# One decode step, forward and backward: attention output and query gradient in one pass over the cache slots

## The chip, the core and the metric

The kernel runs on one core of a Trainium2 chip. The metric is the time of one execution on the device in microseconds (us). The kernel before takes 334.01 us in the median of three runs (333.45 to 334.48). The execution that the profiler recorded spans 335.7 us; all stage times below are from it.

## The reference

A decode step with one new token for each of B = 4 sequences: attention over a cache and a gated feed-forward layer, added to the input, and then all gradients. Cut to what matters:

```python
xn = layernorm(x)                                   # x: [4, 1, 512]
# A: attention over the last W = 1024 of 4096 cache slots, 32 query heads on 8 key/value heads
q = (xn @ wq).reshape(B, 1, 32, 128).transpose(0, 2, 1, 3)
k = repeat(k_cache[:, :, Sk - W:, :], 4, axis=1)    # caches: [4, 8, 4096, 128]
v = repeat(v_cache[:, :, Sk - W:, :], 4, axis=1)
p = softmax(einsum("bhqd,bhkd->bhqk", q, k) * 128 ** -0.5)
o = einsum("bhqk,bhkd->bhqd", p, v)                 # contraction over the slots
a = o.transpose(0, 2, 1, 3).reshape(B, 1, 4096) @ wo
# B: feed-forward, F = 1792
f = (gelu(xn @ w_gate) * (xn @ w_up)) @ w_down
out = x + a + f
# outputs: out and the gradients of x, k_cache, v_cache, wq, wo, w_gate, w_up, w_down for grad_out
```

All arrays are bf16. The gradients of the two caches are zero outside the last 1024 slots, and those zeros have to be written too. In the backward pass `dq` is a contraction over the slots, as `o` is: `dq = dS @ k`, with `dS` the gradient of the scores. The weight gradients are outer products with a contraction over the four sequences only: `dwo` from `o` and `grad_out`, `dwq` from `xn` and `dq`, and those of the feed-forward layer from its rows and `grad_out` or `xn`.

## The kernel before

The kernel first does the feed-forward layer, and then four steps t = 0 to 3 of GP = 2 key/value heads each (HG = 8 query heads). A scheduler of the framework orders each engine's instructions; the program below gives the priorities. Weight gradients and cache gradients are cut into pieces that wait in a list `bg`; `tick(n)` takes the next n of them at fixed places between other work.

```python
J, JQ, rep = 32, 8, 4          # 1024 slots of 4 sequences: 32 blocks of 128 rows per key/value head

od_ps = ps_a.tile([P, 2, GP, Dh], FP32, name="od_ps")     # kept for the whole kernel
# copies of grad_out and of xn, row p kept only where its head of four is i
for src, dst in ((dy_b, dym), (xn_b, xnm)):
    for i in range(rep):
        nc.vector.tensor_scalar(out=dst[:, i, :], in0=src[:], scalar1=msk_i[:, i:i + 1], ...)
...
def scores(t, k):                      # k = 0: S = q k^T;  k = 1: dP = do v^T
    for g in range(GP):
        for q in range(NQ):
            # 8 transposes of 128x128 into T_ps, one copy T_sb, and then
            for b in range(B):         # four PE column groups
                nc.tensor.matmul(ps[b * RG:(b + 1) * RG, :], lhsT=lf[:, b, s * RG:(s + 1) * RG],
                                 rhs=T_sb[:, :, b], ..., tile_position=(0, b * RG))
            tick(2)
...
def by_batch(src, nm):                 # spreads 256 columns over 4 sequences: 1024 columns, on GpSimd
    dst = attw.tile([P, JQ, P], BF16, name=nm, ...)
    nc.gpsimd.tensor_tensor(out=..., in0=src[:].unsqueeze(2).broadcast_to([P, WQ, B]),
                            in1=bmsk[:].unsqueeze(1).broadcast_to([P, WQ, B]), op=ALU.mult)
# softmax:   P_b -> P_x = by_batch(P_b)  -> eight transposes pT_ps -> copy PT
# softmax_d: dS_b -> dS_x = by_batch(dS_b) -> eight transposes pT_ps -> copy dST
...
def odq(t, k):                         # k = 0: o = P v;  k = 1: dq = dS k
    pT, blks = st[t][("PT", "dST")[k]], (v_t, k_t)[k]
    for g in range(GP):
        for j in range(J):
            nc.tensor.matmul(od_ps[0:rep * B, k, g, :], lhsT=pT[:, j % JQ, j // JQ, g], rhs=blks[(t, g)][:, j, :],
                             start=(j == 0), stop=(j == J - 1))
    rows = attw.tile([P, GP, Dh], BF16, name="od_r", ...)
    # k = 0: vector copy of od_ps; k = 1: ScalarE copy with the scale
    # two transposes odT_ps, copy od_T
...
def dw(t):
    # piece_o: dwo of one head: o_r[:, g, :] against dym[:, i, :], 512 columns, 8 pieces
    # piece_q: dwq: two matmuls of 256 columns, xnm against dq_r, 8 pieces
...
def f_rows(srcT, nm):                  # rows of the feed-forward layer, four blocks of 128 per matmul
    ps = od_ps[:].rearrange("p k g d -> p (k g) d")
    for f4 in range(NF4):              # NF4 = 4
        nc.tensor.matmul(ps[0:4 * B, f4, :], lhsT=srcT[:, 4 * f4:4 * f4 + 4, :]..., rhs=ident[:], ...)
    evac(rows[:], ps, 512)
...
for t in range(NT):                    # NT = 4
    if t == 0:
        pre(t)                         # q and do of the step, from transposed wo and from wq
    masks(t)                           # domr, qmr on GpSimd: the right sides of dv and dk
    scores(t, 0)
    softmax(t)
    dvdk(t, 0)                         # puts 16 pieces into the list
    scores(t, 1)
    softmax_d(t)
    dvdk(t, 1)                         # 16 pieces
    odq(t, 0)
    if t + 1 < NT:
        pre(t + 1)
    odq(t, 1)
    fin(t)                             # o @ wo, and dq against transposed wq
    load_next(t)                       # loads of step t + 2
    dw(t)                              # 16 pieces
```

The zeros of the cache gradients (50 MB) are written by large transfers that are issued at fixed places of the program, each behind a ScalarE copy.

Of the kernel before, what the change touches and what calls it, by code (L numbers as in the profile page):

```python
# [14 lines left out]
P = 128  # L15
# [3 lines left out]
def kernel(  # L19
# [113 lines left out]
    msk_i = const.tile([P, rep], FP32, name="msk_i")  # L133
    nc.vector.reduce_sum(out=msk_i[:], in_=ident_f[:].rearrange("p (r b) -> p r b", b=B)[:, 0:rep, :], axis=AX.X)
# [34 lines left out]

    acc = const.tile([P, 2, ND, B], FP32, name="acc")  # L170
# [14 lines left out]
    od_ps = ps_a.tile([P, 2, GP, Dh], FP32, name="od_ps")  # L185
# [27 lines left out]
    xnm = const.tile([P, rep, D], BF16, name="xnm")  # L213
    dym = const.tile([P, rep, D], BF16, name="dym")
    for src, dst in ((dy_b, dym), (xn_b, xnm)):
        for i in range(rep):
            nc.vector.tensor_scalar(out=dst[:, i, :], in0=src[:], scalar1=msk_i[:, i:i + 1], scalar2=None,
                                    op0=ALU.mult)
# [99 lines left out]
    def masks(t):  # L318
        for k, nm in enumerate(("do", "q")):
            mr = attw.tile([P, GP, NQ, Dh], BF16, name=nm + "mr", tag=nm + "mr")  # L320
            nc.gpsimd.tensor_tensor(out=mr[:].rearrange("p g q d -> p (g q) d"),
                                    in0=st[t]["r4"][:, k, :].unsqueeze(1).broadcast_to([P, NS, Dh]),
                                    in1=msk[:].rearrange("p g q -> p (g q)").unsqueeze(2).broadcast_to([P, NS, Dh]),
                                    op=ALU.mult)
            st[t][nm] = mr
# [23 lines left out]
    def by_batch(src, nm):  # L349

        dst = attw.tile([P, JQ, P], BF16, name=nm, tag=nm, bufs=1)
        nc.gpsimd.tensor_tensor(out=dst[:].rearrange("p j (m b) -> p (j m) b", b=B),  # L352
                                in0=src[:].unsqueeze(2).broadcast_to([P, WQ, B]),
                                in1=bmsk[:].unsqueeze(1).broadcast_to([P, WQ, B]), op=ALU.mult)
        return dst
# [12 lines left out]
    def softmax(t):  # L368
# [24 lines left out]
        P_x = by_batch(P_b, "P_x")  # L393
        st[t].update(E=E_f, rr=rr, PT=transposed(P_x, "PT"), P=P_x)

    def softmax_d(t):
        E_f, rr, dP = st[t]["E"], st[t]["rr"], st[t]["dP"]
        Gt = attw.tile([P, WQ], FP32, name="Gt", tag="Gt", bufs=1)
        gs = attw.tile([P, 1], FP32, name="gs", tag="gs")
        nc.vector.tensor_tensor_reduce(out=Gt[:], in0=E_f[:], in1=dP, scale=1.0, scalar=0.0,  # L400
                                       op0=ALU.mult, op1=ALU.add, accum_out=gs[:])
        gs_ps = ps_x.tile([P, 1], FP32, name="gs_ps", tag="x")
        nc.tensor.matmul(gs_ps[:], lhsT=rsum_f, rhs=gs[:], start=True, stop=True)
        cc = attw.tile([P, 1], FP32, name="cc", tag="cc")
        nc.vector.tensor_tensor(out=cc[:], in0=gs_ps[:], in1=rr[:], op=ALU.mult)
        nc.vector.scalar_tensor_tensor(out=Gt[:], in0=dP, scalar=cc[:, 0:1], in1=E_f[:],
                                       op0=ALU.subtract, op1=ALU.mult)
        dS_b = attw.tile([P, WQ], BF16, name="dS_b", tag="dS_b", bufs=1)
        nc.vector.tensor_scalar(out=dS_b[:], in0=Gt[:], scalar1=rr[:, 0:1], scalar2=None, op0=ALU.mult)  # L409
        dS_x = by_batch(dS_b, "dS_x")  # L410
        st[t].update(dST=transposed(dS_x, "dST"), dS=dS_x)

    def odq(t, k):

        pT, blks = st[t][("PT", "dST")[k]], (v_t, k_t)[k]
        for g in range(GP):
            for j in range(J):
                nc.tensor.matmul(od_ps[0:rep * B, k, g, :], lhsT=pT[:, j % JQ, j // JQ, g], rhs=blks[(t, g)][:, j, :],  # L418
                                 start=(j == 0), stop=(j == J - 1))
        rows = attw.tile([P, GP, Dh], BF16, name="od_r", tag=f"od_r{k}")  # L420
        if k == 0:
            nc.vector.tensor_copy(out=rows[:], in_=od_ps[:, k])
        else:
            nc.scalar.activation(out=rows[:], in_=od_ps[:, k], func=ACT.Copy, scale=scale)
        T_ps = ps_w.tile([P, GP, P], BF16, name="odT_ps", tag="w")
        for g in range(GP):
            nc.tensor.transpose(T_ps[:, g, :], rows[:, g, :], ident[:])
        rT = attw.tile([P, GP, rep, B], BF16, name="od_T", tag=f"od_T{k}")
        nc.vector.tensor_copy(out=rT[:],  # L429
                              in_=T_ps[:].rearrange("p g (r b) -> p g r b", b=B)[:, :, 0:rep, :])  # L430
        st[t][("o", "dq")[k]] = rows, rT
# [23 lines left out]
    def dw(t):  # L455

        o_r, dq_r = st[t]["o"][0], st[t]["dq"][0]

        def piece_o(g, i, held):
# [3 lines left out]
            nc.tensor.matmul(mps[:], lhsT=o_r[:, g, :], rhs=dym[:, i, :], start=True, stop=True)  # L463
            evac(held["osb"][:, i, :], mps[:], 512)
            if i == rep - 1:
                r0 = (t * HG + g * rep) * Dh
                store(nc.gpsimd, out=out_5[r0:r0 + rep * Dh, :].rearrange("(h p) n -> p h n", p=P),
                                    in_=held["osb"][:], kind="rest",
                          apart=["zeros", "rest"])

        def piece_q(c2, k, held):
            if k == 0:
                held["osb"] = outp.tile([P, 2, GP, rep, Dh], BF16, name="osb_q", tag="o")
            ci, i2 = k // 2, k % 2
            c = c2 * 2 + ci
            mps = ps_w.tile([P, 2, GP, Dh], FP32, name="dwq_ps", tag="w")
            for i in range(2):
                nc.tensor.matmul(mps[:, i].rearrange("p g d -> p (g d)"),  # L478
                                 lhsT=xnm[:, i2 * 2 + i, c * P:(c + 1) * P],
                                 rhs=dq_r[:].rearrange("p g d -> p (g d)"), start=True, stop=True)  # L480
            evac(held["osb"][:, ci, :, i2 * 2:(i2 + 1) * 2, :], mps[:].rearrange("p i g d -> p g i d"), 512)
            if k == 3:
                store(nc.gpsimd, out=out_4[c2 * 2 * P:(c2 + 1) * 2 * P, t * CW:(t + 1) * CW].rearrange("(c p) j -> p c j", p=P),
                    in_=held["osb"][:].rearrange("p c g i d -> p c (g i d)"), kind="rest",
                          apart=["zeros", "rest"])

        assert rep == 4
# [4 lines left out]
        for c2 in range(ND // 2):  # L492
            held = {}
            for k in range(4):
                bg.append(lambda c2=c2, k=k, held=held: piece_q(c2, k, held))

    def fin(t):

        oT, dqT = st[t]["o"][1], st[t]["dq"][1]
# [16 lines left out]
    NF4 = (NF + 3) // 4  # L516
# [9 lines left out]
    def ftb(name):  # L526
        t_ = ffn.tile([P, 4 * NF4, B], BF16, name=name)
        nc.vector.memset(t_[:], 0.0)
        return t_
# [53 lines left out]
    nc.vector.tensor_tensor(out=aT_b[:, 0:NF, :], in0=gl[:], in1=hu, op=ALU.mult)  # L583
    dhuT_b = ftb("dhuT_b")
    nc.vector.tensor_tensor(out=dhuT_b[:, 0:NF, :], in0=da[:], in1=gl[:], op=ALU.mult)
# [3 lines left out]
    nc.vector.tensor_tensor(out=dhgT_b[:, 0:NF, :], in0=dhg_f[:], in1=gp[:], op=ALU.mult)  # L589
# [3 lines left out]
    def f_rows(srcT, nm):  # L593

        ps = od_ps[:].rearrange("p k g d -> p (k g) d")
        for f4 in range(NF4):
            nc.tensor.matmul(ps[0:4 * B, f4, :], lhsT=srcT[:, 4 * f4:4 * f4 + 4, :].rearrange("p f b -> p (f b)"),
                             rhs=ident[:], start=True, stop=True)
        rows = const.tile([P, NF4, P], BF16, name=nm)
        evac(rows[:], ps, 512)  # L600
# [3 lines left out]
    def piece_d(f4, i, n, held):  # L604
# [3 lines left out]
        nc.tensor.matmul(mps[:], lhsT=a_r[:, f4, :], rhs=dym[:, i, :], start=True, stop=True)  # L608
        evac(held["osb"][:, i, :], mps[:], 512)
        if i == n - 1:  # L610
            store(nc.gpsimd, out=out_8[4 * f4 * P:(4 * f4 + n) * P, :].rearrange("(h p) n -> p h n", p=P),
                                in_=held["osb"][:, 0:n, :], kind="rest",
                      apart=["zeros", "rest"])

    def piece_g(s_r, og, c, i, held):
        if i == 0:
            held["osb"] = outp.tile([P, NF4, 4, P], BF16, name="osb_g", tag="o")
        n = (NF - i + 3) // 4
        mps = ps_w.tile([P, NF4, P], FP32, name="dwg_ps", tag="w")
        nc.tensor.matmul(mps[:, 0:n, :].rearrange("p f d -> p (f d)"), lhsT=xnm[:, i, c * P:(c + 1) * P],  # L620
                         rhs=s_r[:, 0:n, :].rearrange("p f d -> p (f d)"), start=True, stop=True)
        evac(held["osb"][:, 0:n, i, :], mps[:, 0:n, :], n * P)
        if i == 3:
            store(nc.gpsimd, out=og[c * P:(c + 1) * P, :],
                                in_=held["osb"][:].rearrange("p f i d -> p (f i d)")[:, 0:F], kind="rest",
                      apart=["zeros", "rest"])

    for f4 in range(NF4):
        held = {}
        n = min(4, NF - 4 * f4)  # L630
        for i in range(n):
            bg.append(lambda f4=f4, i=i, n=n, held=held: piece_d(f4, i, n, held))
# [3 lines left out]
    for srcT, wsb, og, nm in ((dhgT_b, wg_sb, out_6, "dhg_r"), (dhuT_b, wu_sb, out_7, "dhu_r")):  # L636
        s_r = f_rows(srcT, nm)
        for c in range(ND):
            held = {}
            for i in range(4):  # L640
# [20 lines left out]
    with tc.tile_pool(name="stage", bufs=3, reuse_waits="tile") as stage, \  # L661
# [6 lines left out]
        for t in range(NT):  # L668
# [10 lines left out]
            odq(t, 0)  # L679
# [3 lines left out]
            odq(t, 1)  # L683
# [67 lines left out]
```

## Time and profile before

| | us or share |
|---|---|
| time, median of 3 | 334.01 (333.45 to 334.48) |
| recorded span | 335.7 |
| TensorE (PE) busy | 241.3, 72% |
| VectorE (DVE) busy | 160.8, 48% |
| ScalarE (ACT) busy | 115.6, 34% |
| GpSimd (POOL) busy | 62.8, 19% |
| bytes moved by DMA | 112.38 MB, mean 335 GB/s |
| P_x of the four steps begins at | 73.8, 136.5, 201.2, 266.6 |
| dS_x of the four steps begins at | 97.9, 161.1, 225.2, 290.7 |
| last zeros issued, landing after | 320.85, 12.0 |

P_x is made once a step in the middle of the step, and dS_x once near its end, so the two rows of starts cut each step into two parts: from P_x to dS_x (the second scores, with the matmuls of `o` among them), and from dS_x to the next P_x (the matmuls of `dq`, the preparation of the next step, the closing sums, the first scores, the softmax). In the profile a row of the chain is a start in us, a duration in us, an engine and what it writes; "x64" counts the instructions merged into the row. PEld is the load of the stationary operand, PEclk the granted TensorE clock as a share of the full one.

### The profile page before, as it was taken

To read this page: it belongs to the slowest core of one execution; us is meant where nothing else is said; L and a number is where in the kernel's file an instruction comes from. 1 tells how busy PE (TensorE), PEld (TensorE's weight loads), DVE (VectorE), ACT (ScalarE), POOL (GpSimd) and SP (SyncE) were. 2 spreads that over 40 slices of the span, in tenths; PEclk is the share of its full clock that TensorE was granted. 3 is DMA by queue.
4 is the path that set the end of the run, shared out by engine and by line. 5 is a ranking of instruction groups with operands and counts; after the bars stand their busy time and mean duration, and the time that the engine had idled before them with its cause. 6 is when DMAs were issued, how large, how long until landed. Compare 5 with 4: busy or idle time off the path is not lost. (4 is left out here: it accounts for less than half of the span.)

```text
span 335.7 us, 6838 instructions
## 1 busy us (share of the span) xinstructions
PE 241.3 (72%) x2968; PEld 170.5 (51%) x2968; DVE 160.8 (48%) x310; ACT 115.6 (34%) x219; POOL 62.8 (19%) x77
## 2 busy tenths in 40 slices
PE   0779885628958998498399956956899389469820
PEld 0778762315636864365277535734675166366310
DVE  7465732335336366344426645353366353336860
ACT  3005553333323265224034641330446333106710
POOL 5001123220020502200204122111050400200300
PEclk9966995955985999679787995985979859769955
DMA  7999999996993399999916999999339959971895
GB/s 232 404 386 419 396 374 411 429 427 277 411 377 130 132 316 411 429 423 425 425 75 204 334 427 426 423 424 431 154 127 375 401 234 394 430 297 47 346 394 216
DMA packets 22013, 112.38 MB, mean 335 GB/s; under 512 B 1560, under 2 KB 7712, under 8 KB 13792
## 3 DMA queue, kind: packets, MB, share of 16 engines
q10 hardware_dynamic: 4624, 50.46, 35.8%
q1 hardware_dynamic: 11600, 30.81, 24.5%
q0 software_dynamic: 5760, 30.67, 23.2%
q8 instruction: 23, 0.38, 0.4%
q14 instruction: 6, 0.05, 0.0%
HBM read 30.93 MB, written 81.01 MB: 333 GB/s over the span
## 5 line engine op out<-in xcount | busy, mean ns | idle before, releaser
L96 DVE COPY T_sb<-T_ps 128x1024 bf16<-128x1024 bf16 x64 | 44.3, 692 | 31.8 <-PE T_ps L336 31.0
L94 ACT CAST stg_dv<-kv_ps 128x512 bf16<-128x512 f32 x54 | 29.9, 589 | 64.2 <-PE kv_ps L444 62.6
L94 ACT CAST stg_dk<-kv_ps 128x512 bf16<-128x512 f32 x46 | 25.5, 588 | 16.2 <-PE kv_ps L444 13.6
L336 PE MATMUL T_ps<-ident,vb 128*128 128x128 bf16 x256 | 27.7, 257 | 3.6 <-DVE PT L96 3.3
L336 PEld LDWEIGHTS <-vb 128*128 128x128 bf16 x256 | 21.4, 117 | 12.7 <-issue 10.0
L94 ACT CAST osb_q<-dwq_ps 128x512 bf16<-128x512 f32 x24 | 13.0, 590 | 33.7 <-PE dwq_ps L478 25.2
L336 PE MATMUL T_ps<-ident,kb 128*128 128x128 bf16 x256 | 23.8, 223 | 0.4 <-ACT stg_dk L94 0.4
L336 PEld LDWEIGHTS <-kb 128*128 128x128 bf16 x256 | 17.7, 99 | 11.0 <-issue 5.7
L444 PE MATMUL kv_ps<-domr,P_x 128*128 128x512 bf16 x64 | 22.5, 409 | 1.0 <-DVE od_T L429 1.0
L94 ACT CAST osb_g<-dwg_ps 128x512 bf16<-128x512 f32 (+1 forms) x30 | 14.8, 535 | 23.9 <-PE dwg_ps L620 13.1
L444 PE MATMUL kv_ps<-qmr,dS_x 128*128 128x512 bf16 x64 | 21.4, 411 | 0.6 <-ACT stg_dv L94 0.2
L96 DVE COPY woT<-woT_ps 128x1024 bf16<-128x1024 bf16 x16 | 11.0, 690 | 20.7 <-PE woT_ps L288 20.7
L418 PE MATMUL od_ps<-kb,dST 128*16 128x128 bf16 x256 | 19.6, 245 | 0.0
L418 PEld LDWEIGHTS <-dST 128*16 128x16 bf16 x256 | 17.4, 102 | 2.0 <-issue 1.9
L96 DVE COPY PT<-pT_ps 128x1024 bf16<-128x1024 bf16 x4 | 9.7, 2432 | 14.9 <-PE pT_ps L363 14.9
L418 PE MATMUL od_ps<-vb,PT 128*16 128x128 bf16 x256 | 16.6, 219 | 0.0
L94 ACT CAST osb_o<-dwo_ps 128x512 bf16<-128x512 f32 x24 | 13.2, 588 | 7.7 <-PE dwo_ps L463 7.6
L96 DVE COPY dST<-pT_ps 128x1024 bf16<-128x1024 bf16 x4 | 9.7, 2423 | 12.4 <-PE pT_ps L363 12.4
L418 PEld LDWEIGHTS <-PT 128*16 128x16 bf16 x256 | 14.1, 90 | 2.8 <-issue 2.4
L341 PE MATMUL S_ps<-T_sb,dom 128*32 128x256 bf16 x128 | 12.9, 388 | 3.4 <-DVE T_sb L96 3.4
L100 POOL DMA_DIRECT2D out_dram<-stg_dv x8 | 4.6, 580 | 56.0 <-ACT stg_dv L94 56.0
L352 POOL TENSOR_TENSOR dS_x<-dS_b,bmsk 128x1024 bf16<-128x1024 bf16 x4 | 7.5, 1884 | 38.7 <-DVE dS_b L409 38.7
(187 smaller groups left out, 427.1 us busy)
## 6 DMA issues: line engine op xcount, KB each, us to landing
out_dram<-ztile ACTq DMA_DIRECT2D x8, 3072.0 KB, 15.4
out_dram<-ztile ACTq DMA_DIRECT2D x16, 1536.0 KB, 12.9
kb<-in_A_k_cache_dram SPq DMA_DIRECT2D x8, 1024.0 KB, 14.8
vb<-in_A_v_cache_dram SPq DMA_DIRECT2D x8, 1024.0 KB, 24.2
out_dram<-stg_dv POOLq DMA_DIRECT2D x8, 1024.0 KB, 5.9
out_dram<-stg_dk POOLq DMA_DIRECT2D x8, 1024.0 KB, 8.3
wo_sb<-in_A_wo_dram SPq DMA_DIRECT2D x4, 1024.0 KB, 7.4
wq_sb<-in_A_wq_dram SPq DMA_DIRECT2D x4, 1024.0 KB, 9.4
```

The lines of the kernel that those rows point to most:

```text
L94: last.append(nc.scalar.copy(out=out, in_=in_))
L96: return nc.vector.tensor_copy(out=out, in_=in_)
L100: d = eng.dma_start(out=out, in_=in_)
L336: nc.tensor.transpose(T_ps[:, jj, :], blks[(t, g)][:, q * JQ + jj, :], ident[:])
L341: nc.tensor.matmul(ps[b * RG:(b + 1) * RG, :], lhsT=lf[:, b, s * RG:(s + 1) * RG], rhs=T_sb[:, :, b], start=(g == 0 and q == 0), stop=(g = ...
L352: nc.gpsimd.tensor_tensor(out=dst[:].rearrange("p j (m b) -> p (j m) b", b=B), in0=src[:].unsqueeze(2).broadcast_to([P, WQ, B]), in1=bmsk[ ...
L418: nc.tensor.matmul(od_ps[0:rep * B, k, g, :], lhsT=pT[:, j % JQ, j // JQ, g], rhs=blks[(t, g)][:, j, :], start=(j == 0), stop=(j == J - 1))
L444: nc.tensor.matmul(mps[:].rearrange("p q d -> p (q d)"), lhsT=src[:, jj, :], rhs=mr[:, g].rearrange("p q d -> p (q d)"), start=True, stop= ...
```

## The change

`o` and `dq` are made in one pass over the slots. Each of the four products (two key/value heads, `o` and `dq`) gets its own group of 32 columns of the PE array, so that the four streams of a slot block can be in the array side by side. All four results then lie in one tile of 128 partitions, and one copy, one transpose and one copy follow instead of two chains. Of these rows, GpSimd makes one copy per head that keeps only this head's rows (`X`), and both `dwo` and `dwq` take it as an operand; the eight masked copies of `grad_out` and `xn` are gone, and `dwq` is one matmul of 512 columns per piece instead of two of 256. The spreading of `dS` over the sequences moves from GpSimd to VectorE. The pass comes after the preparation of the next step in the program. The feed-forward rows are held on four partitions (one per sequence) instead of sixteen, which takes one matmul per block of 128 and four copies per row tensor. Some buffers change: the masked right sides `domr` and `qmr` have one buffer instead of two, and the feed-forward rows go through the general PSUM pool.

```diff
+    sc_od = const.tile([P, 1], FP32, name="sc_od")       # 1 for the rows of o, the scale for those of dq
...
-    od_ps = ps_a.tile([P, 2, GP, Dh], FP32, name="od_ps")
+    od_ps = ps_a.tile([P, Dh], FP32, name="od_ps")
...
-    xnm = const.tile([P, rep, D], BF16, name="xnm")
-    dym = const.tile([P, rep, D], BF16, name="dym")
-    for src, dst in ((dy_b, dym), (xn_b, xnm)):
-        for i in range(rep):
-            nc.vector.tensor_scalar(out=dst[:, i, :], in0=src[:], scalar1=msk_i[:, i:i + 1], scalar2=None,
-                                    op0=ALU.mult)
+    for dst, src, own, other in ((dyz, dy_b, slice(0, HP), slice(HP, P)), (xnz, xn_b, slice(HP, P), slice(0, HP))):
+        nc.vector.tensor_copy(out=dst[own, :], in_=src[own, :])
+        nc.vector.memset(dst[other, :], 0.0)
...
-            mr = attw.tile([P, GP, NQ, Dh], BF16, name=nm + "mr", tag=nm + "mr")
+            mr = attw.tile([P, GP, NQ, Dh], BF16, name=nm + "mr", tag=nm + "mr", bufs=1)
...
-        P_x = by_batch(P_b, "P_x")
+        P_x = by_batch(P_b, "P_x", nc.gpsimd)
...
-        dS_x = by_batch(dS_b, "dS_x")
+        dS_x = by_batch(dS_b, "dS_x", nc.vector)
...
+    def odq(t):
+        for j in range(J):
+            for k in range(2):
+                for g in range(GP):
+                    pT, blks, r0 = st[t][("PT", "dST")[k]], (v_t, k_t)[k], (GP * k + g) * (P // 4)
+                    nc.tensor.matmul(od_ps[r0:r0 + rep * B, :], lhsT=pT[:, j % JQ, j // JQ, g],
+                                     rhs=blks[(t, g)][:, j, :], start=(j == 0), stop=(j == J - 1),
+                                     tile_position=(0, r0))
+        rows = attw.tile([P, Dh], BF16, name="od_r", tag="od_r")
+        nc.vector.tensor_scalar(out=rows[:], in0=od_ps[:], scalar1=sc_od[:, 0:1], scalar2=None, op0=ALU.mult)
+        T_ps = ps_w.tile([P, P], BF16, name="odT_ps", tag="w")
+        nc.tensor.transpose(T_ps[:], rows[:], ident[:])
+        rT = attw.tile([P, 2, GP, rep, B], BF16, name="od_T", tag="od_T")
+        nc.vector.tensor_copy(out=rT[:]..., in_=T_ps[:]...)
+        X = attw.tile([P, HG, Dh], BF16, name="od_x", tag="od_x", bufs=1)
+        nc.gpsimd.tensor_tensor(out=X[:], in0=rows[:].unsqueeze(1).broadcast_to([P, HG, Dh]),
+                                in1=hmsk[:].unsqueeze(2).broadcast_to([P, HG, Dh]), op=ALU.mult)
...
-            nc.tensor.matmul(mps[:], lhsT=o_r[:, g, :], rhs=dym[:, i, :], start=True, stop=True)
+            nc.tensor.matmul(mps[:], lhsT=X[:, g * rep + i, :], rhs=dyz[:], start=True, stop=True)
...
-            for i in range(2):
-                nc.tensor.matmul(mps[:, i].rearrange("p g d -> p (g d)"),
-                                 lhsT=xnm[:, i2 * 2 + i, c * P:(c + 1) * P],
-                                 rhs=dq_r[:].rearrange("p g d -> p (g d)"), start=True, stop=True)
+            nc.tensor.matmul(mps[:], lhsT=xnz[:, c * P:(c + 1) * P],
+                             rhs=X[:, g * rep:(g + 1) * rep, :].rearrange("p i d -> p (i d)"), start=True, stop=True)
...
     def f_rows(srcT, nm):
-        for f4 in range(NF4):
-            nc.tensor.matmul(ps[0:4 * B, f4, :], lhsT=srcT[:, 4 * f4:4 * f4 + 4, :]..., rhs=ident[:], ...)
-        evac(rows[:], ps, 512)
+        for f0 in range(0, NF, 4):                        # NF = 14
+            ps = ps_w.tile([P, 4, P], FP32, name="fr_ps", tag="w")
+            for f in range(n):
+                nc.tensor.matmul(ps[0:B, f, :], lhsT=srcT[:, f0 + f, :], rhs=ident[:], start=True, stop=True)
+            evac(rows[0:B, f0 * P:(f0 + n) * P], ps[0:B, 0:n, :]..., n * P)
...
             dvdk(t, 1)
-            odq(t, 0)
             if t + 1 < NT:
                 pre(t + 1)
-            odq(t, 1)
+            odq(t)
             fin(t)
```

## The prediction, made before the changed kernel was seen

> **What bounds the kernel now.** I read the page first, then the chain of work that ended last in order of time, then the timeline round the matmuls that the change touches, then the waits. The page's slices show two things that can bound: DMA and PE.
>
> ```profile
> PE   0779885628958998498399956956899389469820
> PEclk9966995955985999679787995985979859769955
> DMA  7999999996993399999916999999339959971895
> ```
>
> Up to slice 9 (some 84 us) DMA is full: loads and the first stores. After that it has holes in each step (the digits 3, 1, 3, 5, 1), so it waits for compute there. 112.38 MB at the 425 GB/s of full slices would be 264 us, so DMA alone isn't the bound of the last 250 us. PE is not full either, so the bound must be a chain. Its end (t = 3):
>
> ```profile
> 280.75 2.40 PE od_ps L418 x41
> ...
> 290.21 0.36 DVE dS_b L409
> 290.62 0.08 issue
> 290.72 1.89 POOL dS_x L352
> 292.62 0.05 issue
> 292.66 1.05 PE pT_ps L363 x8
> 293.74 2.43 DVE dST L96
> 296.21 0.37 PE odT_ps L427 x2
> 296.58 5.27 PE od_ps L418 x64
> 301.87 0.39 ACT od_r L424
> 302.26 0.05 issue
> 302.31 0.28 PE odT_ps L427 x2
> 302.59 0.79 PE acc_ps L181 x32
> ```
>
> The reader is to see that everything here is in series on one dependency chain: dS_x, the transposes, dST, 64 matmuls of dq, the row copy. The `o` matmuls (first line) are on it too: the scheduler put them among the second scores, where PE is full: over 277 to 284 us the table of windows gives PE 7.00 of 7.00 us.
>
> How much they cost: `o` of t = 2 is two rows of the chain, 10 in 0.66 us and 54 in 3.11 us, so 57.6 ns each (clock 1.00 there). dq of t = 3 is 64 in 5.27 us, 82.3 ns each (clock 0.68). `o` of t = 3 is 0.21+0.38+0.06+0.88+2.40 = 3.93 us, dq of t = 2 is 0.74+1.59+2.55 = 4.88 us. So a step pays about 3.8 + 5.0 = 8.8 us for the two passes.
>
> The timeline shows what column groups do already, in the scores:
>
> ```profile
> 284.85 0.40 PE L341 MATMUL S_ps<-T_sb,dom 128*32 128x256 bf16 x4 [0.51 <-DVE T_sb L96]
> 285.17 0.45 PEld L336 LDWEIGHTS <-vb 128*128 128x128 bf16 x8 [0.22 <-issue]
> 285.18 0.62 PE L336 MATMUL T_ps<-ident,vb 128*128 128x128 bf16 x8
> ```
>
> Four matmuls of 256 columns in four column groups: the next work begins 0.33 us after the first of them. At 57.6 ns per 128 columns they'd need 4 x 115 = 461 ns in series, so they do overlap; about 115 ns of stream and 0.22 us before the next weight load.
>
> **What the Trainium skill says.** "TensorEngine Tiling (Array Packing)", Key Properties: column tiles work independently, and a change of tiling mode drains the array. The 0.22 us above fits such a drain. "TensorE: Matmul & The Clock Gate", Part 3, Measured speedup: a pack takes one matmul plus about 4 ns for each further tile, with 2.38x measured for three column tiles; the four score matmuls above agree in kind. "VectorE: DVE Perf Modes", errata section: an fp32 two-input operation takes (N+151)/0.96 ns; dx_b, 512 wide, took 693 ns against 691. I use it for dS_x too, whose broadcast bf16 operands I expect to gain nothing. "GPSIMD Engine Reference", Engine selection: two-input elementwise work is about 2x slower on GpSimd; here dS_x took 1.88 us for 1024 columns.
>
> **The change part by part**, per step of four.
>
> 1. *The od passes.* Before: 128 matmuls, 8.8 us. After: 32 rounds of four groups. One round is the longer of two things. Stream: 57.6 ns at full clock, 82 ns or more at the lower one. Issue: the narrow acc_ps matmuls run 32 pairs of weight load and matmul in 0.79 us, 24.7 ns a pair, so four pairs are 99 ns. I take 105 ns (estimate): 32 x 0.105 = 3.4 us. If the scheduler still slots the `o` half early into the scores, two groups at a time, it is 1.9 us there and 1.9 to 3.4 us after dST, 3.8 to 5.3 us in all. I take a saving of 4.9 us, all on the path, since both passes are on the chain.
> 2. *dS_x on VectorE*: (1024+151)/0.96 = 1.22 us against 1.89, and about 0.08 us of handing over saved: 0.75 us, on the path.
> 3. *One row copy, transpose and od_T copy* of 128 columns instead of two chains: at the end of the chain 0.39 (od_r) becomes about 0.28 (estimate), 0.28 (odT) about 0.2; some 0.2 us. Fewer mode changes in the scores: `o` of t = 3 sat in five bursts; perhaps one or two drains of 0.22 us. Together 0.4 us.
> 4. *dwo and dwq*: before 8 x 512 + 16 x 256 columns, after 16 x 512, the same; copies out of PSUM unchanged in number. X is new on POOL, about 1.9 us (as domr, 1.89), but dwo comes 10 us later at t = 3. Nothing on the path.
> 5. *One buffer for domr and qmr*: qmr of the next step must wait for the last dk piece, at 256 us instead of 247 for t = 3; it is used only in the step after the softmax. It can hold a store on POOL by 2 us. Nothing on the path.
> 6. *Feed-forward*: 42 matmuls instead of 12 (30 x 58 to 82 ns, about 2.1 us), 12 copies instead of 3 (9 x 0.6 us, spread on ACT and DVE), up to nine more mode changes there and back; less 8 x 0.35 us of masked copies on DVE. PE is 18.4 of 20 us busy over 20 to 40 us, so I expect +2 us at 42 us. Three waits for stores follow (5.6, 5.2 and 2.0 us), which DMA sets; some of the 2 us may vanish there.
>
> Per step: 4.9 + 0.75 + 0.4 = 6.05 us. In t = 1 a wait for a store lies where `o` ran (below), so 4 us there. Sum: 6 + 4 + 6 + 6 = 22 us; less 2 us (feed-forward) and 1 us given back to DMA: 19 us. 334 - 19 = 315 us. The end after the last copy (about 14 us: zeros issued at 320.85, 12.0 us to landing) shifts as it is.
>
> **Rivals.**
> - *The groups don't overlap with new weights each round.* In the scores each group gets one weight load per 256 columns; here one per 128, in 32 rounds on end, which no stage of the kernel before does. Then the passes cost as before and only parts 2, 3 and 6 are left: 334 - 4.6 + 2, about 331 us. Against it: in the old pass weights are already loaded behind the running stream at 57.6 ns.
> - *Stores and zeros become the bound.* A step moves about 23 MB, 54 us at 425 GB/s, in a period of 65 us that would become 59. Output buffers are three deep:
>
> ```profile
> ACT osb_q L94 <- DMA out_dram<-osb_o: 8.5, 2, 5.2
> ```
>
>  One such wait is in t = 1 (5.2 us, while `o` ran), one in the tail. If each step got one, half the gain would go: about 324 us.
> - *More is gained.* After dS_x, PE waited for dST at the head of its queue with the transpose of the `o` rows (odT_ps, 7.5 us in three waits). That transpose now comes later, so the next step's wo transposes can fill the 2.4 us of dST, as in part happened at t = 0. That would be up to 2 us more in three steps: about 308 us.
> - *The feed-forward part or the single buffers cost more than thought*, 6 to 8 us: about 320 us.
>
> **Range and chances.** The chain is clear and the saving on it large against 2% (6.7 us); to miss it, the overlap has to fail or two rivals have to join. What I can't see is the scheduler's new order. Predicted 315 us, 305 to 326 eight times in ten. Faster by over 2%: 0.85; within 2%: 0.12; slower by over 2%: 0.03.
>
> **What would show it right or wrong.** Right: od_ps in the chain 4 us or less a step; no `o` bursts in the second scores, or short ones; dS_x on DVE near 1.2 us; P_x to dS_x down from 24.1 to some 20 us, dS_x to P_x down from 41 to some 39; P_x of t = 0 within 3 us of 73.8. Wrong: od_ps still 7 us or more a step; waits of ACT or DVE on stores in every step; PE waiting for the feed-forward rows; a dS_x of 2 us on DVE, as the strided copies PT and dST take 2.4 us for the same number of columns.

## The result, and the profile after

| | before | after |
|---|---|---|
| time, median (lowest to highest) | 333.73 us (331.13 to 334.48), 4 runs | 320.41 us (317.70 to 323.50), 4 runs |
| ratio | 1 | 0.9587, 95% interval 0.9473 to 0.9701 |
| recorded span, granted clock | 335.7 us, 0.814 | 321.8 us, 0.789 |

The recorded executions of the changed kernel and of the kernel before without zeros (below) are the slowest of their four, so their stages add up to some 3 us more than the medians. The change is worth 13 us; 19 were predicted, and 320.4 lies inside the range of 305 to 326.

Three rows of the page of the changed kernel, in 40 slices of the span as before:

```profile
PE   0769986938759894857499938647898487378710
PEclk9966997765967999577697978696899559558965
DMA  6999999999995799999639999999639969952895
```

The holes of DMA are shallower than before. The last ten digits of the granted clock read 9559558965, where before they read 9859769955: in this execution the end of the kernel runs at half clock for longer. Not all of that belongs to the change: in the recording of the changed kernel with dS_x on GpSimd (below), which takes the same time, they read 9789579965. The pass at t = 3 runs at half clock there too, in 3.58 us.

The chain of the changed kernel at the end of t = 3 (start, us, engine, what it writes; "issue" is time in which the engine waited for nothing that the profile shows), which answers the chain of before:

```profile
274.92 1.24 DVE dS_x L367
276.15 0.05 issue
276.20 1.05 PE pT_ps L378 x8
277.25 0.02 issue
277.27 2.43 DVE dST L96
279.70 0.04 issue
279.74 3.60 PE od_ps L434 x125
...
283.44 0.36 DVE od_r L438
283.80 0.05 issue
283.85 0.30 PE odT_ps L440
...
284.42 1.01 PE acc_ps L196 x32
...
293.56 0.81 PE acc_ps L196 x26
```

One pass of 3.60 us holds both products (before: 3.9 us of `o` among the scores and 5.27 us of dq here), and dS_x takes 1.24 us on VectorE instead of 1.89. But from the first acc_ps to the end of the last (the closing sums of `fin`) it is 9.95 us, where it was 6.12 (302.59 to 308.71).

The timeline of the changed kernel round the start of that pass, and then the waits for a store (osb_q and osb_o are output buffers; in us, the sum, the number and the longest):

```profile
279.92 0.32 PE L434 MATMUL od_ps<-kb,dST 128*16 128x128 bf16 x2
279.92 0.32 PE L434 MATMUL od_ps<-vb,PT 128*16 128x128 bf16 x2
280.02 0.32 PE L434 MATMUL od_ps<-kb,dST 128*16 128x128 bf16 x2
280.03 0.32 PE L434 MATMUL od_ps<-vb,PT 128*16 128x128 bf16 x2
```

```profile
ACT osb_q L94 <- DMA out_dram<-osb_o: 15.5, 3, 6.5
```

A round of four begins every 0.107 us at a clock of 0.50, its four matmuls within 0.01 us of each other: the four streams are in the array together. At t = 0 the same pass runs at a clock of 1.00 with 0.056 us a round, 2.3 us in three bursts; at t = 1 and 2 it is 3.5 us, mostly at half clock. The waits of ScalarE for an output buffer have gone from 8.5 us in two places to 15.5 us in three.

The two rows of starts cut the span into stages. All spans here are from one recorded execution each; the rows from the third on are the experiments below.

| us | to P_x(0) | P_x to dS_x, t = 0..3 | dS_x to next P_x, t = 0..2 | dS_x(3) to end |
|---|---|---|---|---|
| before | 73.8 | 24.2 24.6 24.0 24.1 | 38.5 40.1 41.4 | 44.9 |
| after | 69.2 | 21.4 25.8 23.5 21.8 | 36.8 37.8 38.8 | 46.8 |
| after, one group | 69.2 | 20.7 24.0 23.6 21.1 | 41.0 41.6 43.5 | 50.2 |
| after, halves | 67.8 | 22.6 23.6 21.8 20.9 | 35.8 36.1 37.3 | 46.7 |
| after, dS_x on GpSimd | 68.1 | 21.4 25.0 23.3 19.8 | 37.0 38.5 38.0 | 46.6 |
| before, four buffers | 65.1 | 23.7 23.8 23.9 24.0 | 38.0 40.4 41.5 | 44.7 |
| after, four buffers | 64.9 | 19.4 22.1 20.6 19.7 | 41.0 38.8 39.4 | 45.2 |
| before, o held back | 71.5 | 23.2 24.0 23.0 19.9 | 37.1 37.6 38.5 | 43.1 |
| before, two groups | 72.8 | 22.2 23.4 22.2 21.2 | 37.1 39.7 40.7 | 44.5 |
| before, no zeros | 65.0 | 19.8 19.7 20.2 19.5 | 36.0 37.1 36.0 | 37.6 |
| after, no zeros | 64.7 | 19.4 20.0 20.0 20.0 | 34.6 34.3 34.7 | 36.0 |
| halves, held back, four buffers | 65.0 | 21.3 20.7 18.9 19.7 | 35.7 37.4 35.5 | 44.7 |

The difference of the two spans, 13.9 us, is 4.6 before P_x(0), 4.4 in the four second scores, 6.8 in the three stretches to the next P_x, less 1.9 lost at the end.

### The profile page after: what moved, and what is told of

It reads as the page before. It is cut to its first block, busy times and chain, and to the rows that moved or that the text cites. A ratio compares the mean times of both kernels' runs of the same rounds, so it can differ in the third digit from the quotient of the medians.

```text
span 321.8 us, 6824 instructions
## 1 busy us (share of the span) xinstructions
PE 227.2 (71%) x2954; PEld 151.5 (47%) x2954; DVE 169.5 (53%) x312; ACT 115.8 (36%) x219; POOL 67.7 (21%) x80
## 3 DMA queue, kind: packets, MB, share of 16 engines
q10 hardware_dynamic: 4624, 50.46, 37.3%
## 4 chain that ended last, share of the span: by engine, by line
PE 47%; DMA 23%; DVE 16%; issue 5%; ACT 4%; POOL 2%; ACTq 1%; SPq 0%; DVEq 0%; POOLq 0%
DMA out_dram<-osb_o 14%; PE kv_ps L461 9%; PE T_ps L351 8%; PE S_ps L356 4%; PE od_ps L434 4%; DMA out_dram<-osb_d 3%; PE wqT_ps L521 3%; DVE dST L96 3%; DMA out_dram<-osb_g 3%; DMA wd_sb<-in_B_w_down_dram 3%; PE acc_ps L196 3%; PE wgT_ps L656 2%; PE woT_ps L303 2%; DVE T_sb L96 2%; PE pT_ps L378 2%
## 5 line engine op out<-in xcount | busy, mean ns | idle before, releaser
L351 PE MATMUL T_ps<-ident,vb 128*128 128x128 bf16 x256 | 30.1, 273 | 7.9 <-DVE PT L96 3.3
L351 PEld LDWEIGHTS <-vb 128*128 128x128 bf16 x256 | 23.5, 125 | 21.3 <-issue 19.8
L461 PE MATMUL kv_ps<-domr,P_x 128*128 128x512 bf16 x64 | 25.7, 472 | 1.1 <-DVE wqT L96 1.1
L461 PE MATMUL kv_ps<-qmr,dS_x 128*128 128x512 bf16 x64 | 21.1, 405 | 0.4
L446 POOL TENSOR_TENSOR od_x<-od_r,hmsk 128x1024 bf16<-128x1024 bf16 x4 | 7.5, 1882 | 54.3 <-DVE od_r L438 54.3
L96 DVE COPY PT<-pT_ps 128x1024 bf16<-128x1024 bf16 x4 | 9.7, 2434 | 14.9 <-PE pT_ps L378 14.9
L303 PE MATMUL woT_ps<-ident,wo_sb 128*128 128x128 bf16 x128 | 12.9, 252 | 5.8 <-DVE dST L96 5.8
L96 DVE COPY wqT<-wqT_ps 128x1024 bf16<-128x1024 bf16 x16 | 11.0, 689 | 7.1 <-PE wqT_ps L521 7.1
L434 PE MATMUL od_ps<-kb,dST 128*16 128x128 bf16 x256 | 12.8, 281 | 2.5 <-DVE dST L96 2.5
L303 PEld LDWEIGHTS <-wo_sb 128*128 128x128 bf16 x128 | 10.3, 114 | 8.7 <-issue 7.9
L100 POOL DMA_DIRECT2D out_dram<-osb_q x8 | 5.8, 731 | 40.6 <-ACT osb_q L94 27.0
L356 PE MATMUL S_ps<-T_sb,qm 128*32 128x256 bf16 x128 | 12.7, 387 | 2.3 <-DVE T_sb L96 2.2
## 6 DMA issues: line engine op xcount, KB each, us to landing
kb<-in_A_k_cache_dram SPq DMA_DIRECT2D x8, 1024.0 KB, 14.7
```

The lines of the kernel that those rows point to most:

```text
L96: return nc.vector.tensor_copy(out=out, in_=in_)
L303: nc.tensor.transpose(wT_ps[:, i, c, :], wo_sb[:, 2 * h2 + i, c * P:(c + 1) * P], ident[:])
L351: nc.tensor.transpose(T_ps[:, jj, :], blks[(t, g)][:, q * JQ + jj, :], ident[:])
L434: nc.tensor.matmul(od_ps[r0:r0 + rep * B, :], lhsT=pT[:, j % JQ, j // JQ, g], rhs=blks[(t, g)][:, j, :], start=(j == 0), stop=(j == J - 1) ...
L446: nc.gpsimd.tensor_tensor(out=X[:], in0=rows[:].unsqueeze(1).broadcast_to([P, HG, Dh]), in1=hmsk[:].unsqueeze(2).broadcast_to([P, HG, Dh]) ...
L461: nc.tensor.matmul(mps[:].rearrange("p q d -> p (q d)"), lhsT=src[:, jj, :], rhs=mr[:, g].rearrange("p q d -> p (q d)"), start=True, stop= ...
```

## The experiments

Ratios are against the kernel before, which ran beside them (medians of seven runs each): 333.06 us beside the first four, 334.07 beside the changed kernel with four buffers, the two without zeros and the one with idle matmuls, 333.67 beside the other four.

### One column group

```diff
-                    nc.tensor.matmul(od_ps[r0:r0 + rep * B, :], ..., start=(j == 0), stop=(j == J - 1),
-                                     tile_position=(0, r0))
+                    nc.tensor.matmul(od_ps[0:rep * B, GP * k + g, :], ..., start=True, stop=True,
+                                     tile_position=(0, 0))
```

> The changed kernel with its 512 od matmuls in the same order, but all four streams in one column group (and every matmul closed by itself, so the sums over the slots are left out). Theory A, the gain is the overlap of the four groups: the pass of a step grows from 3.6 us to 7.4 to 10 us, that is 4 to 6 us a step on the path, less where stores set the pace; 333 to 342 us. Rival B, the pass is limited by issuing its weight loads and the gain is only that it stands in one piece: 320 us as the changed kernel.

Measured: 337.37 us, ratio 1.0132 (1.0062 to 1.0202), 17 us over the changed kernel. This kernel leaves out the sums over the slots. The chain at t = 3 of this kernel:

```profile
286.62 2.43 DVE dST L96
...
289.09 9.26 PE od_ps L434 x126
...
298.44 0.36 DVE od_r L438
...
299.36 0.96 PE acc_ps L196 x32
...
306.59 0.81 PE acc_ps L196 x26
```

The same matmuls in the same order take 9.26 us instead of 3.60. So the groups do overlap with a new stationary operand in each round, and without them the change would be a loss of about 1%: moving `o` behind dST is by itself the wrong way. A second thing is to be read here: after the long pass, acc_ps to acc_ps is 8.0 us, against 9.95 after the short one.

### Halves

`o` for all slots first, then dq, two groups at a time:

```diff
-        for j in range(J):
-            for k in range(2):
+        for k in range(2):
+            for j in range(J):
```

> The changed kernel with the loop over o and dq outside the loop over the slots, so that two groups alternate and the o half may be placed early. Theory A: o goes back among the second scores, in 1.9 us instead of 3.8, and dq after dST takes 1.9 to 3.4 us; P_x to dS_x grows by 1 to 2 us, dS_x to P_x falls by up to 1.5 us; 318 to 323 us in all. Rival B, the one unbroken pass of four is what pays: od_ps in all over 5 us a step and 325 us or more.

Measured: 314.29 us, ratio 0.9442 (0.9368 to 0.9516), some 6 us under the changed kernel and below both theories. Two groups in two passes beat four in one. `o` needs no dST, and the scheduler put it where the first theory said, back among the second scores; at t = 2:

```profile
197.83 1.56 PE L434 MATMUL od_ps<-vb,PT 128*16 128x128 bf16 x49
199.33 0.62 PE L351 MATMUL T_ps<-ident,vb 128*128 128x128 bf16 x8
```

The second scores take 89.0 us over the four steps with it, against 89.5 without it in the kernel with dS_x on GpSimd. (ScalarE waits 4.6 to 5.7 us for a store at t = 1 and again at t = 2 in both.) The gain is in the three stretches behind dS_x, 109.1 us instead of 113.3, where 64 of the 128 matmuls are left behind dST; what each part of it owes to fewer matmuls and what to the clock (0.89 there instead of 0.85) isn't separated. In the rounds of four, only the first two `o` matmuls can run early; everything else stands behind the first dq matmul.

### dS_x back on GpSimd

```diff
-        dS_x = by_batch(dS_b, "dS_x", nc.vector)
+        dS_x = by_batch(dS_b, "dS_x", nc.gpsimd)
```

> The changed kernel with dS_x back on GpSimd. Theory A, it is on the path of each step: 1.89 instead of 1.22 us and a handing over, 0.7 us a step, 2 to 3 us in all; 323 us. Rival B, the step is paced by stores and this is hidden: 320 us.

Measured: 319.89 us, ratio 0.9611 (0.954 to 0.9681), not to be told from the changed kernel. The 0.65 us a step that the chain shows saved don't reach the end of the run.

### The feed-forward part undone

The rows again on 16 partitions by four blocks, with the eight masked copies of `grad_out` and `xn`; the attention part as changed.

```diff
-            for f in range(n):
-                nc.tensor.matmul(ps[0:B, f, :], lhsT=srcT[:, f0 + f, :], rhs=ident[:], ...)
-            evac(rows[0:B, f0 * P:(f0 + n) * P], ...)
+        for f4 in range(NF4):
+            nc.tensor.matmul(ps[0:4 * B, f4, :], lhsT=srcT[:, 4 * f4:4 * f4 + 4, :]..., rhs=ident[:], ...)
+        evac(rows[0:4 * B], ps[0:4 * B], 512)
```

> The changed kernel with the feed-forward rows on sixteen partitions again, with the eight masked copies that they need. P_x of t = 0 begins at 69.2 us in the changed kernel and at 73.8 before. Theory A, the new feed-forward part moves the first stores and loads against each other so that the waits for stores are shorter: P_x of t = 0 goes back to some 73 us and the time rises by 3 to 5 us to 324 us. Rival B, the feed-forward part costs 2 us as I predicted and the early gain is chance of one recording: P_x at 67 to 70 us and 318 us.

Measured: 318.43 us, ratio 0.9528 (0.9439 to 0.9617), with P_x(0) at 70.6 us. The feed-forward part is neither a cost nor a measurable gain.

### Four output buffers, after and before

```diff
-    outp = ctx.enter_context(tc.tile_pool(name="outp", bufs=3))
+    outp = ctx.enter_context(tc.tile_pool(name="outp", bufs=4))
```

To make room, the fp32 `xn` is made again at the end; in the kernel before, `domr` and `qmr` also get one buffer each.

> The changed kernel with four output buffers instead of three (to make room, the fp32 xn gives up its place and is made again at the end, about 1 us of VectorE). Theory A, stores that hold up the copies took back part of the gain in the steps t = 1 and 2: the three waits of ScalarE on a store of an output buffer (15.5 us in all, the longest 6.5) fall under 8 us, dS_x of t = 1 comes 3 to 6 us after where it was relative to P_x (25.8 to some 21 us), and the time is 313 to 317 us. Theory B, the waits only move to a later place because the store queues themselves are behind: 318 to 322 us.

> The kernel before with four output buffers instead of three (room as in the run of the changed kernel with four, and one buffer for domr and qmr). Theory A, the waits on stores are something that the shorter steps brought on: the gain here is 2 us or less, 331 to 334 us. Theory B, they cost the kernel before as much (it has two waits of ScalarE, 8.5 us in all, and three in the feed-forward layer, 12.7 us): 6 us or more, 328 us or less.

Measured: 314.39 us after (ratio 0.941, 0.9335 to 0.9485) and 326.18 us before (0.9788, 0.9694 to 0.9883). Neither recorded execution has a wait of ScalarE for osb_q on a store any more. For the changed kernel the first theory held, 6 us; for the kernel before it fell: 7.5 us there too. So the waits on stores cost both kernels alike, and they are not where 6 us of the expected gain went. But they sat in different places. The kernel before wins 8.7 us ahead of P_x(0) and 1.5 in the second scores. The changed one wins 4.3 us ahead of P_x(0) and 10.6 us in the second scores, and gives 5.8 back in the stretches to the next P_x; 2.2 us of that is one gap inside the pass of t = 0, in which PE waits for nothing that the profile shows. With four buffers in both, the change is worth 11.8 us. The second scores then take 81.9 us after and 95.4 before: the 14 us that were expected of that stage are there once no store stands in it.

### Without the zeros

```diff
     def zeros(n):
+        return
```

> The kernel before with the writing of the zeros (50 MB) left out; its cache gradients are not zero outside the window. With the next run it shows what the change is worth when stores are few. Theory A, compute chains bound both: 310 to 325 us here. Theory B, the stores set the pace: under 300 us.

> The changed kernel with the zeros left out in the same way. Theory A, the change is worth the predicted 19 us or more in compute and the stores took some 6 us back: this kernel is 18 to 25 us faster than the kernel before without zeros. Theory B, what is missing lies in the compute chain itself (clock, order): the distance is 13 us or less, as with the zeros.

Both leave out the 50 MB of zeros. Measured: 289.77 us before (287.13 to 292.58) and 286.22 after (285.48 to 287.69), so the change is worth 3.5 us here, which is of the size of the runs' spread. Leaving out the zeros brings 44 us before and 34 us after. The first run came out where its second theory put it; of the pair's theories on the change the first fell: with less to store, the gain should have grown. The stage table shows why: the second scores of the kernel before now take 19.5 to 20.2 us, as those of the changed kernel do, though nothing in the code of `o` has changed. The timelines show where it stands. The kernel before with zeros at t = 2:

```profile
212.86 0.40 PE L341 MATMUL S_ps<-T_sb,dom 128*32 128x256 bf16 x4
213.19 0.39 PE L478 MATMUL dwq_ps<-od_r,xnm 128*128 128x256 bf16 x2
213.51 3.18 PE L418 MATMUL od_ps<-vb,PT 128*16 128x128 bf16 x54
216.63 0.62 PE L336 MATMUL T_ps<-ident,vb 128*128 128x128 bf16 x8
```

and without:

```profile
195.09 0.40 PE L343 MATMUL S_ps<-T_sb,dom 128*32 128x256 bf16 x4
195.30 0.74 PE L420 MATMUL od_ps<-vb,PT 128*16 128x128 bf16 x10
196.13 0.38 PE L405 MATMUL gs_ps<-gs,rsum 128*128 128x1 f32 x2
196.44 2.79 PE L420 MATMUL od_ps<-vb,PT 128*16 128x128 bf16 x47
```

With the zeros the scheduler put 54 matmuls of `o` ahead of the next score transposes, in the middle of the chain. Without them 47 stand behind the last scores, where PE waits for the softmax gradient anyway. So this pair changes two things, the stores and the order, and what it points to is the order. That led to the next run.

### The kernel before with o held back

A matmul of one column that reads gs, row sums that the softmax gradient takes from the finished second scores, is put ahead of each `o` pass. Nothing else is changed: one column group, GpSimd for dS_x, three output buffers.

```diff
         for g in range(GP):
+            if k == 0:
+                nc.tensor.matmul(od_ps[0:rep * B, k, g, 0:1], lhsT=ident_f[:, 0:rep * B],
+                                 rhs=st[t]["gs"][:], start=True, stop=True)
             for j in range(J):
```

> The kernel before, with one matmul of a single column that reads gs put ahead of each o pass, so that o can't start before the last scores are done; it is then 33 matmuls while PE waits for dS_x and 31 while it waits for dST, still in one column group. Theory A, a good part of the change's gain is the order (the scheduler of the kernel before put 54 matmuls of o ahead of the score transposes): P_x to dS_x falls from 24.2 to 20.5 to 21.5 us, dS_x to the next P_x grows by at most 1.5 us, and the time is 321 to 328 us. Theory B, the gain is the column groups alone, and o takes PE as long wherever it stands: 331 to 336 us.

Measured: 317.63 us (316.62 to 319.80), ratio 0.9542 (0.9457 to 0.9627): as much as the whole change, or more, from the order of 64 matmuls. The theory's total was beaten, its stages were not met: P_x to dS_x came down by 0.9, 0.6 and 1.0 us where about 3 were expected, and by 4.2 at t = 3. At t = 1 and 2 ScalarE waits 5.6 and 5.0 us for a store there, as in the changed kernel (13.8 us in three places, the third at the end); at t = 0 it doesn't, and why so little was gained there isn't shown. The stretch to the next P_x didn't grow, it fell by 1.5 to 2.9 us: 6.9 us in all, where the second scores gave 6.6. The chain at t = 3 of this kernel:

```profile
277.61 2.43 DVE dST L96
280.03 0.26 DVE od_r L426
280.30 0.05 issue
280.34 0.29 PE odT_ps L431 x2
280.63 3.68 PE od_ps L422 x64
```

dq has not changed, and takes 3.68 us instead of 5.27: 57.5 ns a matmul. Rows of the table by stretch of time (stretch, its length, busy time of PE, of the PE loads, DVE, ACT and POOL, PEclk, DMA share, GB/s), of the changed kernel, then of this one, each over the pass and the closing sums of t = 3:

```profile
280.00:284.00 4.00, 3.48 (x127) 3.17 (x116) 0.35 (x1) 0.00 (x0) 0.05 (x1) 0.50 0.94 390
284.00:292.00 8.00, 6.32 (x63) 4.26 (x62) 2.15 (x5) 2.25 (x4) 2.38 (x2) 0.51 0.34 138
```

```profile
280.00:284.00 4.00, 3.66 (x64) 3.56 (x65) 0.46 (x3) 0.00 (x0) 0.00 (x0) 1.00 1.00 418
284.00:291.00 7.00, 6.27 (x111) 4.58 (x110) 3.62 (x7) 4.42 (x9) 0.10 (x1) 1.00 0.50 204
```

With `o` in the time in which PE waited for dS_x and dST, PE has work there, the clock is full when dST is ready, and it stays full: 0.97 over the three stretches from dS_x to the next P_x, against 0.83 to 0.87 before. What of the 16 us is the place of `o` and what the clock behind it isn't separated, since one edit brought both. The Trainium skill, "TensorE: Matmul & The Clock Gate", Part 1, says that TensorE falls to half its clock after an idle window of some 3.4 us and comes back after one of work, with 107 and 56 ns from one matmul of 128 columns to the next. Here the rounds of four come at 107 ns at a clock of 0.50 and the matmuls of dq at 57.5 ns at 1.00. On the spacings the trace agrees; the length of the idle window was not tested.

### Idle matmuls in the waits of the changed kernel

27 matmuls of 256 columns a step whose results nothing reads, 9 on P_b, 6 on dS_b and 12 on dS_x:

```diff
+        fp = filler(6, dS_b[:], None)
         dS_x = by_batch(dS_b, "dS_x", nc.vector)
         st[t].update(dST=transposed(dS_x, "dST"), dS=dS_x)
+        filler(12, dS_x[:, 0:2, :].rearrange("p j m -> p (j m)"), fp)
```

> The changed kernel with idle matmuls of 256 columns (27 a step, nothing reads them) while TensorE waits for P_x and for dS_x and dST, which keep the granted clock up. Theory A, the shorter pass and the idle time ahead of it leave the clock at one half for what follows: the pass takes 2.3 to 2.7 us instead of 3.5, the closing sums after the last pass about 6 us instead of 9.8, and the time falls by 4 to 8 us, to 312 to 316. Theory B, other waits set the end: 318 to 322 us. Theory C, the fillers delay the real matmuls: over 323 us.

Measured: 315.19 us, ratio 0.9416 (0.9347 to 0.9486), mean clock 0.881 instead of 0.79 to 0.81. The time is what the first theory said, 5 us less for work that does nothing. Its parts are only half right. From the first dq matmul to od_r it is 3.8, 3.0, 3.1 and 4.0 us in the four steps, against 3.8, 4.2, 4.3 and 3.7, and the closing sums still take 10.0 us; the clock falls to one half again at 276 us, just as they begin (acc_ps at 275.22).

### The kernel before with two groups a pass

Column groups alone: the two heads side by side in each pass, the order left to the scheduler.

```diff
-        for g in range(GP):
-            for j in range(J):
-                nc.tensor.matmul(od_ps[0:rep * B, k, g, :], ...)
+        for j in range(J):
+            for g in range(GP):
+                nc.tensor.matmul(od_ps[32 * g:32 * g + rep * B, k, g, :], ..., tile_position=(0, 32 * g))
```

> The kernel before with its two key/value heads side by side in two column groups in each of the two passes, everything else as it was (the row copies are unchanged, so the sums of the second head lie in rows that the later steps don't read). Theory A, overlap is worth what it saves on each pass: o 1.9 us instead of 3.7 and dq 3.3 instead of 5.0, some 3.5 us a step, 319 to 322 us. Theory B, half of it is lost because what surrounds the passes sets the pace: 325 to 330 us.

Measured: 325.13 us, ratio 0.9766 (0.969 to 0.9842); the sums of the second head are not read in this kernel. That is 8.5 us where the first theory said 12 to 15, in the range of the second. The scheduler put `o` into the same place as before (at t = 2, 49 of its 64 matmuls in one burst), and the second scores give 7.9 us, what a pass of 1.9 us instead of 3.7 was to give. What is missing lies behind dST. At t = 3 dq takes 3.54 us instead of 5.27, but the closing sums take 7.8 instead of 6.1. And 3.54 us for two groups, with the clock at one half, is hardly less than the 3.68 that one group takes at full clock in the kernel with `o` held back.

### Halves, o held back, four output buffers

What the runs so far point to, in one kernel: the loop order of the halves, the matmul on gs ahead of it, and the fourth buffer.

> The changed kernel with o and dq as two halves of two groups each, o held back as in the first run of this call, and four output buffers: what the runs so far point to. If the gains of the halves (6 us) and of the buffers (6 us) add up: 306 to 310 us. If both remove the same wait: 312 to 316 us.

Measured: 301.68 us (298.46 to 303.02), ratio 0.904 (0.8931 to 0.9149). It beats both kernels, by 32 and by some 19 us, and does better than the sum that was expected. Its timeline at t = 2, and its chain at t = 3:

```profile
197.46 0.38 PE L418 MATMUL gs_ps<-gs,rsum 128*128 128x1 f32 x2 [0.65 <-DVE gs L415]
197.77 0.21 PE L432 MATMUL od_ps<-gs,ident_f 128*16 128x1 f32 x4
197.84 1.73 PE L438 MATMUL od_ps<-vb,PT 128*16 128x128 bf16 x56
200.27 0.62 PE L378 MATMUL pT_ps<-ident,dS_x 128*128 128x128 bf16 x8 [0.70 <-DVE dS_x L367]
```

```profile
256.15 2.43 DVE dST L96
258.58 0.04 issue
258.63 1.98 PE od_ps L438 x64
```

56 matmuls of `o` in 1.73 us, all inside the wait for dS_x, and then dq in 1.98 us: two groups at full clock, 31 ns a matmul. PE still waits 0.70 us for dS_x, so `o` costs nothing there. Work in the wait doesn't make the clock certain, though: at t = 1 it falls just as dq begins, and 43 matmuls of dq take 2.5 us at 0.50 (147.83 to 150.35 us). Against the changed kernel with four buffers the halves and the matmul on gs bring 12.7 us together (314.39 to 301.68); neither was run alone with four buffers.

## Why the prediction was right or wrong

The time was right and the range held it, with errors in the steps that partly cancelled.

1. **The od passes (4.9 us a step).** The length of the pass came out, 3.5 to 3.6 us at t = 1 to 3 against 3.4, but by luck: 105 ns a round was worked out from the issue of four pairs, and the measured 107 ns is the half clock. At full clock (t = 0) a round takes 56 ns, little more than half of what the prediction held for the limit. "All on the path, since both passes are on the chain" is the step that failed. The 3.8 us of `o` were on the chain only because the scheduler had put them in front of the score transposes: held behind gs in the old kernel they run in PE's wait (at t = 3 the stage is 4.2 us shorter, about the length of `o`), and that kernel has the time of the changed one. In the changed kernel the stage from P_x to dS_x gave 4.4 us over the four steps where 14 were expected (24.1 to some 20 us a step), 21.4, 25.8, 23.5 and 21.8. I had seen the wait for a store under `o` at t = 1 and took 2 us off for it. That term was mis-sized: without `o` to fill it the wait at t = 1 is 6.5 us and a second one of 5.7 us stands at t = 2, and with a fourth buffer the same stage is 10.6 us shorter.
2. **dS_x on VectorE (0.75 us on the path).** 1.24 us instead of 1.89, as worked out, and on the chain in the trace; but put back on GpSimd it changes nothing that can be measured. Being a row of the chain was not enough.
3. **The row copies and transposes (0.4 us).** od_r 0.36 and odT 0.30 against 0.39 and 0.28 before: no gain here.
4. **dwo, dwq and the copies X.** X takes 1.88 us on GpSimd and lies beside other work, as said.
5. **One buffer for domr and qmr.** GpSimd waits for it, and the old kernel with single buffers and a fourth output buffer got faster, not slower. No cost is seen in these runs, though it was never undone by itself.
6. **Feed-forward (+2 us).** The sign was wrong, and little hangs on it: P_x(0) came 4.6 us sooner, of which the undone part keeps 3.2 (70.6), while the times of the two kernels can't be told apart. With four buffers P_x(0) is at 65 us in either kernel. That stage is set by waits on stores, as the prediction suspected for "some of the 2 us", not by the 42 matmuls.

The stretch from dS_x to the next P_x came as predicted, 2.3 us less in the mean; part of that is luck too, since with four buffers in both kernels all three stretches together are only 0.7 us shorter (2.9 without the gap of 2.2 us). "The end after the last copy shifts as it is" held too: 14.9 us before and 14.7 after. What was not foreseen lies between: from dS_x(3) to the end, parts 1 to 3 were to save some 2 us, and 1.9 were lost. The pass was done 2.6 us sooner, but the closing sums took 3.8 us more. Half of that goes with the clock: in the changed order with one group, where the longer pass has brought the clock up, they take 8.0 us at full clock instead of 9.95. The other 1.9 us, against the 6.1 of before, are waits of PE for VectorE's copies inside the sums: 0.26, 0.78, 0.57 and 0.31 us in the kernel with one group, for acc once and wqT three times, where the kernel before waits 0.20 us once. The changed kernel without zeros has no more of them than that, and its sums take 6.3 us at full clock, so they don't belong to the fused pass as such; why the changed kernel has them only with zeros wasn't traced.

Of the rivals, "the groups don't overlap" is shown wrong by the kernel with one group. "Stores become the bound" was right about the place, the second scores, and wrong about what it says of the change: the old kernel pays as much for three buffers, in the feed-forward layer. "More is gained, as the next step's transposes can fill the 2.4 us of dST" names the thing that mattered, work in PE's wait. But the wo transposes didn't fill it, they stand waiting for dST themselves (5.8 us in three places); it was `o` that fitted there, and the rounds of four tie it to dST. That the clock then decides what a pass costs had no place among the rivals, although the prediction used 57.6 and 82 ns side by side.

What stays open: why the fillers brought 5 us when the pass and the closing sums explain only part of it, how the gain of the held-back `o` divides between its place and the clock, and what the kernel before without zeros owes to the order and what to the missing stores, since both changed together.

## What to carry to other kernels

Before work on the chain is made faster, ask why it is on the chain: the 64 matmuls of a step here could move into a wait behind a gating matmul of one column, and that was worth as much as the whole change. Fuse passes only if the fused one doesn't tie early work to late data; here two half passes, the first in the wait and the second after it, beat one dense pass by 12.7 us, with four output buffers in both. And read the granted clock by stage: a shorter burst after an idle time can run at half clock, so that what it saves in columns it pays in nanoseconds.

## What the runs showed of the hardware that was not expected

- Rounds of four column groups, each with four new stationary operands, cost no more than one matmul: 55 to 60 ns a round at full clock (t = 0 of the changed kernel, and the run with idle matmuls), 107 ns at half. I had taken the issue of four pairs, 99 ns, for the limit; at full clock it is not. In "TensorE: Matmul & The Clock Gate", Part 3, the Trainium skill gives some 4 ns for each further tile; the four starts within 0.01 us agree. The limit that I took from acc_ps, 24.7 ns a pair, doesn't hold here.
- The same pass has a hole of 1.7 us in the recorded run with idle matmuls, between 272.2 and 273.9 us at a clock of 1.00, with no wait that the profile shows. The changed kernel with four buffers has one of 2.2 us in the pass of t = 0 (up to 100.17 us, from 97.9), at the same clock. DMA is full in both (417 to 455 GB/s). Where they come from isn't shown.
- While zeros are written, DMA moves 425 to 427 GB/s over a whole second-scores stage (t = 1 and 2, both kernels), and a store of one output buffer can take 20 us from issue to landing (20.06 us on the chain of the changed kernel at t = 1; the median of its eight stores of osb_o is 15.1 us).
